# Attention scores from 32-row tiles instead of 64-row tiles with zero queries

## The chip, the cores and the metric

The kernel runs on one core of one Trainium2 chip. The metric is the device time of one execution in microseconds (us). Before the change it is 827.35 us, the median of three runs (826.49 to 828.32). A profile is one such execution, recorded instruction by instruction.

The engines are named as the profile names them: PE is TensorE (matmuls; PEld its weight loads), DVE is VectorE, ACT is ScalarE, POOL is GpSimd, SP is SyncE, which issues most DMAs. PE multiplies a stationary operand (the weights, here up to 128 rows by 128 columns) with a moving operand of up to 512 columns, and writes into PSUM. The array can be split: a matmul with a tile position uses only some rows (a row tile) or only some columns (a column tile), and matmuls on different rows or columns can run at the same time.

## The reference

The input x has 2048 rows of 512 numbers, in bf16. The result is a mix, row by row, of an attention block and a feed-forward block:

```python
def _A_ref(x, wqkv, wo):                       # H = 32 heads, Dh = 16
    qkv = (x @ wqkv).reshape(B, S, 3, H, Dh).transpose(2, 0, 3, 1, 4)
    q, k, v = qkv[0], qkv[1], qkv[2]
    scores = jnp.einsum("bhqd,bhkd->bhqk", q, k) * (Dh ** -0.5)
    p = softmax(scores, axis=-1)
    o = jnp.einsum("bhqk,bhkd->bhqd", p, v)
    return o.transpose(0, 2, 1, 3).reshape(B, S, D) @ wo

def _B_ref(x, w_gate, w_up, w_down):           # 1792 hidden columns
    return (silu(x @ w_gate) * (x @ w_up)) @ w_down

g = sigmoid((x * gate_w).sum(-1, keepdims=True))
return g * a + (1 - g) * b
```

32 heads of 2048 x 2048 scores make 134 million exponentials; that is most of the work outside of PE.

## The kernel before

**Units and tiles.** A unit is four heads (a group g of 8) times one block of 512 queries (qb of 4): 32 units, in the order of the list UNIT. Keys come in 16 tiles of 128 (KT). For one unit and one tile of keys there are four score products, one for each head: 128 keys by 512 queries, a full PSUM bank each. A score tile has keys on the partitions, so that the exponentials can go straight into the product with the values.

**The operands of a score product.** The tile kaug holds the keys of a group, four heads in four strips of 32 partitions: head j in rows 32j to 32j+31. In a strip, row 0 is set to ones, 16 rows hold the head's keys, and the rest is filler that meets zeros. The queries have the same strips; row 0 carries a bound for each query, by which the scores are lowered so that the exponential can't overflow. The queries are stored twice, as variants v = 0 and v = 1 (the second index of q): variant v has the strips of the heads with j % 2 = v, and zeros in the strips of the others. This holds for the tiles q0, q0a, q1 and qx. They are filled in that way by q_pieces, bound_pieces (lines 522 to 611) and variants (575 to 588), none of which the change touches.

**Which products there are.** score (line 719) emits one of them. emit_pair (732) emits two, into the two banks of a tile s_t: heads 0 and 2, or heads 1 and 3 (HEADS at line 717 is 0, 2, 1, 3). ACT then takes the exponential of the whole tile, 128 x 1024, into e_t. There are two s_t tiles in turn. emit_d (765) emits a single one into a tile d_t, in one of three PSUM banks that the rest of the work shares; DVE takes its exponential with a chain of bitwise and arithmetic instructions into y_t, four heads in the order 0, 2, 1, 3. ACT has 841 pairs, DVE 366 single products (91 tiles of keys with all four heads, and two heads of one more).

**The other matmuls.** All the large ones between the scores are split into four column tiles of 128 rows by 32 columns, which run together: the products with the values (pv, line 891, into o_ps), the projections, the feed-forward block (gu, dps, ops). I call four of these one column product. Only two output tiles at the end (two_banks, line 391, tiles a_l_a and a_l_b) use row tiles of 64 rows.

**The order.** Every engine executes in the order in which the program emits (ordered, line 146). That order is laid out while the program is built, by a plan with fixed costs: spend (302) adds 0.216 us to the planned PE time for each pair, single score product or column product, and 0.1 us when the shape changes between rows ("R") and columns ("C"); ACT_US (755) is the planned time of an exponential. In the loop from line 1455 on, the program emits the next pair as soon as its s_t is planned to be free, and fills the time until then with column products and d_t products. Units and their side work have due times (Pacer, 48).

In the profile, every matmul has line 158 (the helper mm), every DVE instruction of the loop line 170, every ACT instruction line 161, so groups are told apart by their tiles: s_t, d_t, e_t, y_t, o_ps and so on.

Of the kernel before, what the change touches and what calls it, by code (L numbers as in the profile page):

```python
# [79 lines left out]
def kernel(  # L80
# [76 lines left out]
    def mm(*args, **kw):  # L157
        return ordered(nc.tensor.matmul(*args, **kw))  # L158
# [360 lines left out]
    def get_q(qb, g):  # L519
        return q1 if g == 1 else qx[(qb * (NB - 1) + g // 2 - 1) % 2][:, :, g % 2, :]  # L520
# [198 lines left out]
    def score(ps, b):  # L719
        n, j = b // 4, HEADS[b % 4]  # L720
        (qb, g), kt = UNIT[n // KT], n % KT
        r = slice(64 * (j // 2), 64 * (j // 2) + 64)
        q = (q0a if n < KT // 2 else q0[qb])[r, j % 2, :] if g == 0 else get_q(qb, g)[r, j % 2, :]
        mm(ps, lhsT=kaug[r, g, kt * P:(kt + 1) * P], rhs=q, start=True, stop=True,
           tile_position=(64 * (j // 2), 0))

    s_end = [0.0, 0.0]
    e_end = {}
# [3 lines left out]
    def emit_pair(bs):  # L732
        i = pairs[0] % 2
        s_t = ps_s.tile([P, 2 * QBW], F32, tag="s", name="s_t")
        e_t = etp.tile([P, 2 * QBW], BF16, tag="e", name="e_t")
        for k, b in enumerate(bs):
            score(s_t[:, k * QBW:(k + 1) * QBW], b)
            e_of[b] = e_t[:, k * QBW:(k + 1) * QBW]
        spend("R", 1, s_end[i])
        flush_act()  # L740
        ready = plan.pe + 0.27

        def exp():
            act(out=e_t[:], in_=s_t[:], func=ACT.Exp, scale=inv_sqrt_dh)
            plan.act = max(plan.act, ready) + ACT_US
            s_end[i] = plan.act + 0.2
            for b in bs:
                e_end[b] = plan.act + 0.27
        exps.append((ready, exp))
        for b in bs:  # L750
            e_left[b] = pairs[0]
        pairs[0] += 1
# [12 lines left out]
    def emit_d():  # L765
# [5 lines left out]
        vcur["i"] += 1  # L771
        d_t = m_tile("d_t")
        score(d_t[:, :], 4 * n + i)
        spend("R", 1)
        e_of[4 * n + i] = y[:, i * QBW:(i + 1) * QBW].bitcast(BF16)
# [819 lines left out]
```

## Time and profile before

| | before |
|---|---|
| median of the runs | 827.35 us (826.49 to 828.32) |
| span of the profiled execution, first to last instruction | 827.2 us |
| ACT busy | 808.9 us (98%) |
| DVE busy | 796.7 us (96%) |
| PE busy | 786.0 us (95%), 8124 matmuls |
| exponentials on ACT (e_t) | 841, mean length 1102 ns |
| score matmuls | 2048, of which 1682 into s_t and 366 into d_t |
| mean granted PE clock | 0.996 |

How to read it: busy time is the time in which at least one instruction of the engine is recorded as running. Neighbouring instructions of an engine overlap in the record, so the busy time of a group is less than its count times its mean length, and the distance from start to start tells what one more of them costs. The length of a matmul has its way through the array in it. The granted clock is the share of PE's full clock that the chip lets through; it is listed with its times. In the list of groups, the number behind the second bar is the idle time of the engine in front of the group's instructions, and behind the arrow stands what ended it. An s_t matmul that waits for ACT e_t waits for its PSUM tile to be read; an e_t that waits for PE s_t waits for its scores.

### The profile page before, as it was taken

Reading aid. Unit: us, or ns where it says so; the run is one execution under the profiler, and the core shown is the slowest. Engines: PE = TensorE matmul, PEld = TensorE weight load, DVE = VectorE, ACT = ScalarE, POOL = GpSimd, SP = SyncE. Lnnn points to the kernel's source line nnn. Section 1 sums busy time; section 2 is a strip of 40 time slices with the busy share of each in tenths; the row PEclk is TensorE's granted clock in tenths of the full one; section 3 lists DMA queues with packets and bytes.
Section 4 is the critical chain, followed back from the end, with each engine's and each line's share of the span. In section 5 each row is a group of like instructions: output and inputs, shape, how many; then the busy total and the mean of one; then the engine's idle time right before and its main releaser. Section 6 shows DMA issues by size and latency. Waiting matters only on the chain. (4 is left out here: it accounts for less than half of the span.)

```text
span 827.2 us, 20410 instructions
## 1 busy us (share of the span) xinstructions
PE 786.0 (95%) x8124; PEld 231.5 (28%) x8125; DVE 796.7 (96%) x1180; ACT 808.9 (98%) x910; POOL 105.5 (13%) x124
## 2 busy tenths in 40 slices
PE   8999999999999999899999999899999999899997
PEld 3322332222222222222222222222222222222222
DVE  6899999999999999999999999999999999999996
ACT  6999999999999999999999999999999999999996
POOL 5010111010111110110111111001011011111110
PEclk9999999999999999999999999999999999999999
DMA  8034346575543445464434555544344545534341
GB/s 178 14 75 90 60 84 125 120 154 104 106 97 64 84 99 126 94 125 94 84 75 90 109 126 110 116 77 95 79 93 88 116 104 115 111 62 83 81 101 48
DMA packets 101095, 79.75 MB, mean 96 GB/s; under 512 B 75744, under 2 KB 89032, under 8 KB 101000
## 3 DMA queue, kind: packets, MB, share of 16 engines
q0 software_dynamic: 12960, 47.19, 30.9%
q1 hardware_dynamic: 86312, 30.93, 15.8%
q8 instruction: 63, 1.03, 0.5%
q10 hardware_dynamic: 1728, 0.33, 0.2%
q14 instruction: 32, 0.26, 0.1%
HBM read 21.55 MB, written 2.35 MB: 29 GB/s over the span
## 5 line engine op out<-in xcount | busy, mean ns | idle before, releaser
L161 ACT ACTIVATE e_t<-s_t 128x1024 bf16<-128x1024 f32 x841 | 784.5, 1102 | 4.1 <-PE s_t L158 3.4
L158 PE MATMUL s_t<-qx,kaug 64*128 64x512 bf16 x1334 | 275.6, 384 | 23.9 <-ACT e_t L161 20.2
L170 DVE TENSOR_SCALAR y_t<-d_t 128x512 uint16<-128x512 f32 x366 | 238.7, 682 | 3.1 <-PE d_t L158 2.4
L158 PEld LDWEIGHTS <-kaug 64*128 64x128 bf16 x2048 | 110.2, 93 | 336.2 <-issue 326.0
L158 PE MATMUL o_ps<-e_t,vaug 128*32 128x512 bf16 x1682 | 168.7, 391 | 0.6 <-DVE osb L170 0.4
L158 PE MATMUL d_t<-qx,kaug 64*128 64x512 bf16 x298 | 101.9, 380 | 2.4 <-DVE y_t L170 0.9
L816 POOL DMA_DIRECT2D y_t<-u_t x45 | 46.8, 1039 | 351.8 <-PE s_t L158 231.7
L158 PEld LDWEIGHTS <-vaug 128*32 128x32 bf16 x2048 | 50.3, 93 | 124.1 <-issue 123.1
L816 POOL DMA_DIRECT2D y_t<-kaug x39 | 41.5, 1063 | 282.5 <-PE s_t L158 145.7
L158 PE MATMUL gu<-xT,wg 128*32 128x512 bf16 x896 | 76.2, 383 | 1.2 <-DMA wg<-in_B_w_gate_dram 0.6
L158 PE MATMUL gu<-xT,wu 128*32 128x512 bf16 x896 | 73.8, 382 | 0.0
L170 DVE TENSOR_SCALAR y_t<-y_t 128x2048 uint16<-128x2048 uint16 x92 | 62.7, 682 | 2.8 <-DMA y_t<-wd_t 1.1
L170 DVE TENSOR_SCALAR z_t<-y_t 128x2048 uint16<-128x2048 uint16 x92 | 63.0, 685 | 1.1
L158 PE MATMUL ops<-wd_t,mt 128*32 128x512 bf16 x672 | 56.7, 383 | 0.0
L170 DVE TENSOR_TENSOR u_t<-u_t 128x2048 f16<-128x2048 f16 (+1 forms) x46 | 55.5, 1207 | 0.9
L170 DVE TENSOR_TENSOR u_t<-u_t,z_t 128x2048 f16<-128x2048 f16 (+1 forms) x46 | 55.4, 1204 | 0.2
L170 DVE TENSOR_TENSOR kaug<-kaug 128x2048 f16<-128x2048 f16 x40 | 48.9, 1221 | 0.9
L170 DVE TENSOR_TENSOR kaug<-kaug,z_t 128x2048 f16<-128x2048 f16 x40 | 48.6, 1216 | 0.1
L158 PE MATMUL s_t<-q,kaug 64*128 64x512 bf16 x208 | 42.3, 383 | 2.7 <-ACT e_t L161 2.4
L170 DVE SCALAR_TENSOR_TENSOR mt<-gs,gu 128x512 bf16<-128x512 bf16 x56 | 38.2, 682 | 2.5 <-PE gu L158 0.2
L170 DVE SCALAR_TENSOR_TENSOR gs<-th,gu 128x512 bf16<-128x512 bf16 x56 | 38.1, 680 | 0.3
L161 ACT ACTIVATE th<-gu 128x512 bf16<-128x512 f32 x56 | 37.4, 668 | 0.0
(148 smaller groups left out, 570.8 us busy)
## 6 DMA issues: line engine op xcount, KB each, us to landing
y_t<-u_t POOLq DMA_DIRECT2D x45, 512.0 KB, 5.0
y_t<-kaug POOLq DMA_DIRECT2D x39, 512.0 KB, 5.0
wg<-in_B_w_gate_dram SPq DMA_DIRECT2D x56, 128.0 KB
wu<-in_B_w_up_dram SPq DMA_DIRECT2D x56, 128.0 KB
y_t<-wd_t POOLq DMA_DIRECT2D x6, 512.0 KB, 5.0
on<-osb SPq DMA_DIRECT2D x120, 16.0 KB
rb<-rr SPq DMA_DIRECT2D x15, 128.0 KB
wd_t<-in_B_w_down_dram SPq DMA_DIRECT2D x7, 256.0 KB
```

The lines of the kernel that those rows point to most:

```text
L158: return ordered(nc.tensor.matmul(*args, **kw))
L161: ordered(nc.scalar.activation(*args, **kw))
L170: return lambda *a, **kw: ordered(f(*a, **kw))
L816: nc.gpsimd.dma_start(out=ya, in_=ua, accum_op=ALU.add)
```

## The change

Each score product takes only the 32 rows of its own head, of the keys and of the queries, and is placed on the row tile of 32 rows at these rows. Before, it took the 64 rows of two heads (heads 0 and 1, or 2 and 3), with zeros in the other head's strip of the queries. The result is the same sum without the zero terms. The queries' variants, their zeros and the DMAs that fill them stay as they are: head j still reads variant j % 2. The pairs, the order and the costs of the plan stay too.

```diff
     def score(ps, b):
         n, j = b // 4, HEADS[b % 4]
         (qb, g), kt = UNIT[n // KT], n % KT
-        r = slice(64 * (j // 2), 64 * (j // 2) + 64)
+        r = slice(32 * j, 32 * j + 32)
         q = (q0a if n < KT // 2 else q0[qb])[r, j % 2, :] if g == 0 else get_q(qb, g)[r, j % 2, :]
         mm(ps, lhsT=kaug[r, g, kt * P:(kt + 1) * P], rhs=q, start=True, stop=True,
-           tile_position=(64 * (j // 2), 0))
+           tile_position=(32 * j, 0))
```

So the two products of a pair lie on rows 0 to 31 and 64 to 95, or on 32 to 63 and 96 to 127, where they took the two halves of the array before.

## The prediction

> **What bounds the kernel now.** I read the busy shares first, then the costliest groups, then who waits for whom, then the matmuls in order of time, and last the granted clock over short stretches. The first two are on the page:
>
> ```profile
> PE 786.0 (95%) x8124; PEld 231.5 (28%) x8125; DVE 796.7 (96%) x1180; ACT 808.9 (98%) x910; POOL 105.5 (13%) x124
> ...
> PEclk9999999999999999999999999999999999999999
> ...
> L161 ACT ACTIVATE e_t<-s_t 128x1024 bf16<-128x1024 f32 x841 | 784.5, 1102 | 4.1 <-PE s_t L158 3.4
> L158 PE MATMUL s_t<-qx,kaug 64*128 64x512 bf16 x1334 | 275.6, 384 | 23.9 <-ACT e_t L161 20.2
> ...
> L158 PE MATMUL d_t<-qx,kaug 64*128 64x512 bf16 x298 | 101.9, 380 | 2.4 <-DVE y_t L170 0.9
> ```
>
> Three engines are full. ScalarE's exponentials set the pace: 841 of them in 784.5 us, 0.93 us each, with 4.1 us of idle time in front of all of them together. So almost nothing can be won in front of ScalarE, but whatever makes the score tiles late is paid there. TensorE is idle for 827.2 - 786.0 = 41 us, much of it by waiting for ScalarE; its order is fixed when the program is built, and the change touches none of the costs from which it is built, so I take the order of instructions as the same.
>
> Next, what a turn of score products costs on TensorE. In the timeline of the matmuls (start, length, operation, count):
>
> ```profile
> 303.13 0.40 PE L158 MATMUL o_ps<-e_t,vaug 128*32 128x512 bf16 x4
> 303.36 0.39 PE L158 MATMUL gu<-xT,wg 128*32 128x512 bf16 x4
> 303.68 0.39 PE L158 MATMUL s_t<-q,kaug 64*128 64x512 bf16 x2
> 304.00 0.40 PE L158 MATMUL gu<-xT,wg 128*32 128x512 bf16 x4
> 304.22 0.60 PE L158 MATMUL gu<-xT,wu 128*32 128x512 bf16 x8
> ```
>
> Read starts, not lengths. Two column products (four tiles of 128 rows by 32 columns) follow each other after 0.22 to 0.23 us. A pair of scores between column products takes 0.32 us on either side: 0.22 of streaming and 0.10 for each change of shape. The pair's two matmuls start together, because they hold different halves of the rows.
>
> Last, the clock. It is full from 5.6 us to the tail except for one stretch. These are three neighbouring stretches of 3.41 us, the length of that gap in the clock (busy us of PE, PEld, DVE, ACT, POOL, then the granted clock), and the matmuls of the first one:
>
> ```profile
> 142.16:145.58 3.42, 2.18 (x16) 0.77 (x15) 3.32 (x7) 3.09 (x4) 0.00 (x0) 1.00 0.07 19
> 145.58:148.99 3.41, 3.41 (x27) 1.04 (x26) 3.34 (x6) 2.46 (x3) 0.99 (x1) 0.50 0.08 20
> 148.99:152.40 3.41, 3.41 (x41) 0.91 (x39) 2.71 (x4) 3.10 (x4) 0.00 (x0) 1.00 0.99 155
> ```
> ```profile
> 142.04 0.39 PE L158 MATMUL s_t<-qx,kaug 64*128 64x512 bf16 x2 [0.25 <-ACT e_t L161]
> 142.37 0.40 PE L158 MATMUL o_ps<-e_t,vaug 128*32 128x512 bf16 x4
> 142.99 0.37 PE L158 MATMUL d_t<-qx,kaug 64*128 64x512 bf16 x1 [0.23 <-DVE gs L170]
> 143.00 0.58 PE L158 MATMUL s_t<-qx,kaug 64*128 64x512 bf16 x2
> 143.79 0.40 PE L158 MATMUL gu<-xT,wg 128*32 128x512 bf16 x4 [0.20 <-DVE mt L170]
> 144.39 0.37 PE L158 MATMUL d_t<-qx,kaug 64*128 64x512 bf16 x1 [0.20 <-DVE y_t L170]
> 144.40 0.58 PE L158 MATMUL s_t<-qx,kaug 64*128 64x512 bf16 x2
> ```
>
> The stretch in which TensorE worked least is followed by one at clock 0.50. The price is in ACT's column: 3.41 - 2.46 = 0.95 us lost in the slow stretch and 3.41 - 3.10 = 0.31 in the next, 1.26 us that a full ScalarE never makes up.
>
> **The change, part by part.** It adds and removes no instruction, DMA or wait. Each of the 2048 score matmuls (1682 into s_t, 366 into d_t) keeps its 512 columns and 128 outputs and goes from 64 rows to 32.
>
> *The duration of one.* No 32-row matmul is in the trace. By rows of other heights: 384 ns (64 rows) and 391 ns (128 rows, o_ps); weight loads 93 ns (64 rows by 128 columns) and 97 ns (128 by 128). Twice the rows cost 7 and 4 ns, so half of them saves 0 to 7 ns; I take 0. A pair still starts together: its heads (0, 2) or (1, 3) lie on different strips.
>
> *Turns within a visit to the score shape.* A d_t product holds half of the rows and must take turns with one of a neighbouring pair: 143.00 shows it, 0.58 us for the pair instead of 0.39. With strips of 32 rows it collides only with its own head. The timeline has 789 visits, of which 282 hold more than one pair or a d_t beside a pair. With the heads as the code deals them out (d_t in the order 0, 2, 1, 3), and no waits, these visits need 1149 turns now and 979 then: 170 x 0.22 = 37 us of TensorE. In the trace, only 99 products start some 0.22 us behind a product of the same half but another strip: 22 us is the value I take, 0 and 37 the ends. The gain falls to an engine that then waits for ScalarE, as s_t already does for 23.7 us in the list of waits. On the end of the kernel it is worth at most what ScalarE loses to s_t, 3.4 us in 7 waits. Of these, 1.6 us (3 waits) lie between 136 and 150 us, around the slow stretch, and I leave them; 1.8 us is the gain, 0 to 3.4 the ends. d_t also comes sooner to VectorE, which waits 2.4 us for it and is 96% busy, beside ScalarE and not behind it: 0.
>
> [...]
>
> [...]
>
> *The filled share of the array, and the clock.* This decides. I laid the 3.41 us grid over the whole trace (the start of the slow stretch and the fall of the clock in the tail, 824.8 us, both lie on it) and summed for each stretch the streaming time, 0.213 us a product, in two ways: as time with any product in the array, and weighted with rows x columns of 128 x 128. A column product and a pair count 1 either way; a lone d_t counts 1 as time and a half as filling. The stretch at 142.16 has 0.41 as time and 0.34 as filling. The lowest stretches after which the clock stayed full have 0.46 as time (346.9 us) and 0.41 as filling (814.5 us). So the clock falls below a limit between 0.41 and 0.46 if time counts, between 0.34 and 0.41 if filling counts; the trace fits both. They part with the change: a pair fills a half instead of all, a d_t a quarter. The mean filling of the 239 stretches goes from 0.66 to 0.52, and 10 stretches come under 0.34, 15 under 0.374 (the middle), 23 under 0.41. One of them is the slow stretch of now, so 9, 14 or 22 are new.
>
> [...]
>
> Between the two ways no row decides. I take filling, because the clock is granted to the array and half of it will carry nothing; that is a judgement, at a little over even. Price of a new slow stretch: 1.26 us measured; the ends are 0.95 (that stretch alone) and 1.71 (half of 3.41, nothing hidden). Sum: 14 x 1.26 = 17.6 us; ends 9 x 0.95 = 8.6 and 22 x 1.71 = 38. What the turns save doesn't help there, since the work that fills the array is the same whoever takes turns; their 1.8 us and the seams' 0.3 I set off within the rounding.
>
> The sum is made against the profiled span, 827.2 us, which is within 0.2 of the median of the runs (827.35, from 826.49 to 828.32), so I add nothing for what lies around it: 827.2 + 17.6 = 845 us, with ends 836 and 865.
>
> **Rivals.** *Time counts, and the strips pay off (faster).* The clock stays, 22 us of turns go, and ScalarE's 1.8 us with them: 827.2 - 1.8 + 0.3 = 825.7, at best 827.2 - 3.4 = 823.8. For it: the 0.20 us turn at 143.00 can be seen, and the waits are there. Against it: ScalarE is full, and shorter turns also shorten the busy time of a stretch. It decides if no stretch falls under 0.41 to 0.46 of time.
>
> *Time counts, and nothing comes of it (same).* The seven waits of ScalarE have other causes, or one or two of the stretches now near 0.50 of time lose a turn (0.22 of 3.41 us is 0.06) and fall under the limit: 827.2 - 1.8 + 1.26 = 826.7; with four of them, 830.4, already slower.
>
> *The 32-row shape costs more for each visit (slower for another reason).* For instance a longer change of shape, or weights that load later. TensorE has 41 us of idle time in 789 visits, so up to 52 ns a visit are covered, and beyond it each visit's excess is paid in full: at 0.10 us, another change of shape, 79 - 41 = 38 us, 865 us. For it: no row shows the shape. Against it: heights of 64 and 128 rows differ by 4 and 7 ns.
>
> **How the numbers follow.** Filling decides, 845 us: 0.52. Another cost of the shape: 0.10. Time counts and faster: 0.18; same: 0.15; slower through new slow stretches: 0.05. Against the bound of 0.2% (1.7 us, about what a measurement of this kernel can tell from no change) that is faster 0.18, same 0.15, slower 0.67. The range goes from 825, which takes in nearly all of the two cases near 827, to 866, the upper ends of both slower cases; what lies outside is the better half of the faster case and a price above these ends.
>
> **What would show it.** Right: the clock at 0.50 in some 10 to 25 stretches of 3.41 us, each behind one with a low filling, and ScalarE's idle time in front of e_t up by about 1 us for each. The turns: pairs beside a d_t of another strip with 0.39 us instead of 0.58, and more time of s_t waiting for ScalarE. Wrong: a full clock behind stretches filled to 0.23 or 0.3, which would make time the measure; or visits of a pair that take more than 0.32 us on either side at full clock, which would be the third rival.

## The result, and the profile after

The changed kernel takes 854.17 us, the median of four runs (850.77 to 859.44), against 827.77 us beside it (826.49 to 828.32): a ratio of 1.033, with a 95% interval from 1.029 to 1.038. The profiled execution took 850.96 us, of which 848.9 are its span, 21.7 us more than the span before. In the ratios here and in the table below, executions that took over 1.5% longer than the fastest of their kernel are left out (one of all32, one of thirdstrip, two of onlypairs32); the medians and ranges have all of them.

From the page of the changed kernel, the lines that answer to those of before (busy us of each engine, its share of the span and its instructions; the granted clock in tenths, in 40 equal slices, where 9 is 0.9 or more; then groups with their count, busy us, mean ns of one, and idle time in front of them):

```profile
PE 799.8 (94%) x8124; PEld 232.2 (27%) x8125; DVE 798.8 (94%) x1180; ACT 813.0 (96%) x910; POOL 103.7 (12%) x124
...
PEclk9999968799989999799999999999999999699999
...
L161 ACT ACTIVATE e_t<-s_t 128x1024 bf16<-128x1024 f32 x841 | 789.1, 1110 | 22.3 <-PE s_t L158 19.4
L158 PE MATMUL s_t<-qx,kaug 32*128 32x512 bf16 x1334 | 272.5, 391 | 30.5 <-ACT e_t L161 28.1
...
L158 PE MATMUL d_t<-qx,kaug 32*128 32x512 bf16 x298 | 101.5, 386 | 3.6 <-DVE y_t L170 0.9
```

The work is the same, instruction for instruction, and none of the groups of 100 and more matmuls grew by more than 34 ns on the mean: s_t from 384 to 391 ns, with the slow stretches in it. But the clock has holes, and ScalarE's idle time in front of e_t has gone from 4.1 to 22.3 us, nearly all of it in wait for s_t. At the same time s_t waits longer for ScalarE than before (28.1 against 20.2 us in this row). TensorE is faster than needed most of the time, and too slow in the holes.

Here is one hole: five neighbouring stretches of the changed kernel (busy us of PE, PEld, DVE, ACT, POOL, then the granted clock; the last two numbers, of the DMA, play no part), and the matmuls of the first of them.

```profile
339.02:342.43 3.41, 2.80 (x26) 0.98 (x26) 3.34 (x6) 3.41 (x5) 0.99 (x1) 1.00 0.66 130
342.43:345.84 3.41, 3.22 (x28) 0.74 (x21) 3.41 (x6) 2.91 (x4) 0.86 (x1) 0.50 0.34 70
345.84:349.26 3.42, 3.42 (x27) 0.62 (x29) 2.75 (x5) 2.93 (x5) 0.00 (x0) 0.50 0.95 163
349.26:352.67 3.41, 3.41 (x34) 0.78 (x28) 1.82 (x2) 1.77 (x2) 0.00 (x0) 0.50 0.39 89
352.67:356.08 3.41, 2.69 (x38) 0.92 (x41) 2.41 (x4) 2.98 (x4) 0.00 (x0) 1.00 0.46 105
```
```profile
339.17 0.39 PE L158 MATMUL s_t<-qx,kaug 32*128 32x512 bf16 x2
340.08 0.39 PE L158 MATMUL s_t<-qx,kaug 32*128 32x512 bf16 x2 [0.53 <-ACT e_t L161]
340.40 0.40 PE L158 MATMUL o_ps<-e_t,vaug 128*32 128x512 bf16 x4
340.74 0.39 PE L158 MATMUL d_t<-qx,kaug 32*128 32x512 bf16 x1
341.00 0.39 PE L158 MATMUL s_t<-qx,kaug 32*128 32x512 bf16 x2
341.32 0.40 PE L158 MATMUL gu<-xT,wg 128*32 128x512 bf16 x4
341.65 0.38 PE L158 MATMUL d_t<-qx,kaug 32*128 32x512 bf16 x1
341.92 0.39 PE L158 MATMUL s_t<-qx,kaug 32*128 32x512 bf16 x2
```

The page calls PE busy for 2.80 of 3.41 us in the first stretch, because its bars overlap (a bar is 0.39 us long where the next product can start after 0.22). By streaming time (0.213 us a product: half of the 0.427 us that lies between the starts of full-size products from 1.7 to 4.2 us of both profiles, where they follow each other at half the later rate) it is 0.56 of the stretch, by filling 0.34, since the four pairs count a half each and the two single products a quarter. The clock falls to 0.50 behind it, and stays there for three stretches. ACT loses 0.50, 0.49, 1.64 and, at full clock again, 0.43 us. The whole execution has 20 slow stretches in front of the tail, in seven holes of 1, 1, 3, 3, 3, 4 and 5. The profiled execution of before had one; of the 25 other executions of it whose mean clock is on record, 24 have 0.999 or 1.000, so most have none.

### The profile page after: what moved, and what is told of

It reads as the page before. It is cut to its first block, busy times and chain, and to the rows that moved or that the text cites. A ratio compares the mean times of both kernels' runs of the same rounds, so it can differ in the third digit from the quotient of the medians.

```text
span 848.9 us, 20407 instructions
## 1 busy us (share of the span) xinstructions
PE 799.8 (94%) x8124; PEld 232.2 (27%) x8125; DVE 798.8 (94%) x1180; ACT 813.0 (96%) x910; POOL 103.7 (12%) x124
## 4 chain that ended last, share of the span: by engine, by line
PE 38%; ACT 29%; DVE 23%; issue 7%; DMA 2%; SPq 0%; DVEq 0%; ACTq 0%
ACT e_t L161 27%; PE s_t L158 13%; DVE y_t L170 9%; PE o_ps L158 7%; PE gu L158 6%; DVE u_t L170 4%; DVE kaug L170 4%; PE d_t L158 4%; PE kp L158 2%; DVE z_t L170 2%; PE ops L158 2%; ACT th L161 2%; DVE mt L170 1%; PE qp L158 1%; DVE gs L170 1%
## 5 line engine op out<-in xcount | busy, mean ns | idle before, releaser
L161 ACT ACTIVATE e_t<-s_t 128x1024 bf16<-128x1024 f32 x841 | 789.1, 1110 | 22.3 <-PE s_t L158 19.4
L158 PE MATMUL s_t<-qx,kaug 32*128 32x512 bf16 x1334 | 272.5, 391 | 30.5 <-ACT e_t L161 28.1
L158 PEld LDWEIGHTS <-kaug 32*128 32x128 bf16 x2048 | 110.4, 91 | 360.0 <-issue 353.1
L158 PE MATMUL o_ps<-e_t,vaug 128*32 128x512 bf16 x1682 | 173.7, 403 | 0.3 <-ACT e_t L161 0.2
L158 PE MATMUL d_t<-qx,kaug 32*128 32x512 bf16 x298 | 101.5, 386 | 3.6 <-DVE y_t L170 0.9
L158 PE MATMUL gu<-xT,wg 128*32 128x512 bf16 x896 | 80.4, 402 | 0.4 <-DMA wg<-in_B_w_gate_dram 0.4
L158 PE MATMUL gu<-xT,wu 128*32 128x512 bf16 x896 | 78.8, 406 | 0.0
L158 PE MATMUL s_t<-q,kaug 32*128 32x512 bf16 x208 | 44.0, 407 | 3.3 <-ACT e_t L161 3.2
```

Source lines behind the costliest of these rows:

```text
L161: ordered(nc.scalar.activation(*args, **kw))
```

## The experiments

Two kinds were run: matmuls by themselves, and the block with parts of the change. The times of the second kind are in the table behind them.

### Matmuls by themselves

**fill**: stages of products with different parts of the array in use.

```diff
+    full(60, "w_a")                       # 128 rows x 128 columns
+    rows(80, 64, (0, 1), "r64x2")         # two row tiles of 64
+    rows(80, 32, (0, 2), "r32x2")         # row tiles of 32: two, then one, three, four
+    cols(80, 32, (0,), "c32x1")           # column tiles of 32: one, then two, four
```

> Not the block: only bf16 products of 512 moving columns, in stages of 80 turns with all 128 rows x 128 columns (filling 1.0) in between; the output is no result of the block. TensorE streams without a pause in every stage, so busy time is 1.0 throughout. Stages and their filling: two row tiles of 64 (1.0), two of 32 (0.5), one of 64 (0.5), one of 32 (0.25), three of 32 (0.75), four of 32 (1.0), one column tile of 128 x 32 (0.25), two (0.5), four (1.0). Theory filling: the clock falls to 0.50 in exactly two stages, one tile of 32 rows and one column tile of 32 columns (0.25 is under the 0.34 to 0.41 of the trace before), and stays full in the others; the turns of a stage go from 0.22 to 0.43 us where it falls. Rival time: the clock stays full throughout, since no stage has an idle TensorE. Rival rows (only the number of active rows counts): it falls with one tile of 32 rows and not with one column tile.

Measured: neither. Each product got a new PSUM tile and so waited for the one before it; one product took 0.64 us from start to start in all stages, and the span was 773.4 us. The page gives a granted clock of 1.00, and that is a trap. The profile before lists 1.00 for its first 5 us too, where products of this size start 0.427 us apart and take up to 634 ns; its first clock entry is at 5.6 us, and behind it, from 7.7 to 9.9 us, they start 0.215 us apart and take 376 to 379. So 1.00 can also mean that no change of the clock is on record, and here none is. The row of the full-size products tells the speed: 583 ns, against 377 to 391 ns in the block, so by their length the clock was at a half from beginning to end (in fill2 below, where its changes are recorded, products of 512 columns follow each other after 0.43 us at half clock and 0.22 at full). A full product every 0.64 us streams 0.213 us at full speed, a third of the time, and the clock did not come up.

```profile
L26 PE MATMUL w_a<-mov 128*128 128x512 bf16 x60 | 35.0, 583 | 6.2 <-DMA mov<-in_A_x_dram 2.8
```

**duty**: k pairs of row tiles, then a wait for ScalarE.

```diff
+    for i in range(k):
+        for j, s in enumerate(strips):
+            mm(ps[j][:, :], lhsT=mov[r, 0:P], rhs=mov[r, :], tile_position=(h * s, 0), ...)
+    nc.scalar.activation(out=junk[:], in_=ps[-1][:, :], func=ACT.Copy)
```

> Not the block either: turns of k pairs of row tiles, then a wait for ScalarE to read the last bank (about 1 us, by the 0.6 to 0.7 us of a 512-column instruction and the ways between the engines), over and over; the output is no result of the block. k pairs stream 0.216 k us. k = 4, 5 and 7 are run with 64 rows and with 32: the same busy time, about 0.46, 0.52 and 0.60 of a turn, at half the filling. Theory filling: with 64 rows the clock holds at k = 4, 5 and 7 (0.46 and more) and falls or wavers at k = 3 (0.39); with 32 rows it falls at k = 4, 5 and 7 (0.23, 0.26, 0.30), still at 10 (0.34), and holds at 20 (0.41), with 14 (0.38) on the edge. Rival time: 32 and 64 rows hold or fall at the same k.

It had the same waits between its products (0.64 us from pair to pair, span 1568.8 us, no change of the clock), so it says nothing on the question. Both were repeated with one PSUM tile for each stage.

**fill2**

> Not the block: the stages of the run fill again, with one PSUM tile for each stage, so that the products stream without waits; the output is no result of the block. TensorE is busy throughout. Filling of the stages: two row tiles of 64 (1.0), two of 32 (0.5), one of 64 (0.5), one of 32 (0.25), three of 32 (0.75), four of 32 (1.0), one column tile of 128 x 32 (0.25), two (0.5), four (1.0), each of 80 turns, with full products in between. Theory filling: the clock falls to 0.50 in exactly two stages, one tile of 32 rows and one column tile (0.25 is under the limit near 0.36), and stays full in the others. Rival time: full throughout, since no stage has an idle TensorE. Rival rows (only the number of active rows counts): it falls with one tile of 32 rows and not with one column tile.

Measured, in the order 32 rows x2, 64 x1, 32 x1, 32 x3, 32 x4, one column tile, two column tiles (busy us of PE, PEld, ACT, POOL, then the clock):

```profile
46.00:61.00 15.00, 15.00 (x143) 7.81 (x139) 0.00 (x0) 0.00 (x0) 1.00 0.01 1
72.00:87.00 15.00, 15.00 (x71) 6.57 (x70) 0.00 (x0) 0.00 (x0) 1.00 0.01 1
102.00:128.00 26.00, 26.00 (x62) 8.97 (x61) 0.00 (x0) 0.00 (x0) 0.50 0.00 0
146.00:161.00 15.00, 15.00 (x213) 8.08 (x210) 0.00 (x0) 0.00 (x0) 1.00 0.00 1
172.00:187.00 15.00, 15.00 (x287) 8.26 (x280) 0.00 (x0) 0.00 (x0) 1.00 0.01 2
199.00:214.00 15.00, 15.00 (x71) 6.78 (x70) 0.00 (x0) 0.00 (x0) 1.00 0.00 0
229.00:244.00 15.00, 15.00 (x142) 7.87 (x140) 0.00 (x0) 0.00 (x0) 1.00 0.00 1
```

TensorE is busy without a pause in every line, and the clock falls in one: single products of 32 rows (third line, 0.50). A single column tile of 128 rows by 32 columns (sixth line, 1.00) has the same area and keeps the clock. So time is refuted, and so is the area that I had written down as filling: in these stages **rows count, columns don't**. In the block the two are the same number, since its column tiles run four at a time; the rival that I had named last is the right form of the theory.

**duty2**

> Not the block: k pairs of row tiles, then a wait for ScalarE to read the last bank, over and over, again with one PSUM tile for each stage; the output is no result of the block. k pairs stream 0.216 k us, the wait adds about 0.95. With 64 rows k is 3, 4, 5, 7 (busy share 0.41, 0.48, 0.53, 0.61, filling the same); with 32 rows 4, 5, 7, 10, 14, 20 (busy 0.48, 0.53, 0.61, 0.69, 0.76, 0.82, filling half of that). Theory filling: with 64 rows the clock holds at all k; with 32 rows it falls at 4, 5 and 7 (0.24, 0.27, 0.31), is on the edge at 10 (0.35) and holds at 14 and 20 (0.38, 0.41). Rival time: both heights hold or fall at the same k.

Measured for k = 7, 64 rows first, then 32:

```profile
185.00:240.00 55.00, 38.20 (x319) 17.36 (x319) 13.71 (x23) 0.00 (x0) 1.00 0.00 1
422.00:502.00 80.00, 65.20 (x290) 23.63 (x291) 12.08 (x21) 0.00 (x0) 0.50 0.00 1
```

The same products for each wait keep the clock with 64 rows and lose it with 32. With 64 rows it held at all four k, down to a share of 0.42 on the average (k = 3: 3 x 0.216 of 1.55 us a turn) and 0.375 in its thinnest stretches of 3.41 us. With 32 rows it fell at all six. That it fell at 14 and 20 too was not expected: on the average they have 0.39 and 0.41, but the falls came behind single thin stretches. One that holds a whole wait of 0.90 us has (3.41 - 0.90) / 3.41 x 0.5 = 0.37 at most; the stretch in front of the fall had 0.364 in both, and with k = 20 it took 17 us until one came. And once down it did not come back: it is 0.50 over the 55 to 112 us that were read of each of the six. Pairs of 32 rows at half clock offer at most a quarter (half of the rows at half the speed, an estimate).

### The block with parts of the change

The kernels of this group share one edit ahead of the loop: the transposed x is made by products with the identity instead of by transposing DMAs. base64 is the kernel before with this edit, all32 the changed kernel with it.

> The kernel before with one difference ahead of the loop, which the three runs beside it share: the transposed x comes from TensorE products with the identity instead of from transposing DMAs. The loop is the same, so this is the base for those three. All theories: 0 to 15 us more than the kernel before, all of it in the first 30 us; the clock full behind that, but for 0 to 3 stretches.

> The whole change on that base. All theories: the difference of the change itself, 22 to 32 us above base64, with 15 to 30 slow stretches of 3.41 us.

| run | median us (range) | ratio to the kernel before [95%] | slow stretches in the loop, profiled execution |
|---|---|---|---|
| base64 | 840.56 (840.19 to 841.44) | 1.016 [1.015, 1.018] | 1 |
| all32 | 864.71 (860.00 to 881.54) | 1.044 [1.040, 1.047] | 16 |
| onlypairs32 | 888.17 (875.58 to 899.91) | 1.066 [1.057, 1.074] | 25 |
| onlysingle32 | 857.39 (856.15 to 858.94) | 1.036 [1.034, 1.038] | 2 |
| warm32 | 851.32 (848.81 to 855.19) | 1.028 [1.026, 1.031] | 10 |
| thirdstrip | 845.00 (843.56 to 856.29) | 1.021 [1.020, 1.022] | 5 |
| thirdstrip64 | 855.74 (851.89 to 861.30) | 1.035 [1.032, 1.038] | 19 |

thirdstrip and thirdstrip64 ran together on another chip than the other five; the kernel before took 827.82 us beside them, against 826.80 beside base64 and all32.

The base costs 13.8 us more than the kernel before (840.56 against 826.80 beside it), and the change on it 24.2 us, close to the 26.4 us of the change itself. So the base is good for comparisons.

**onlypairs32**

```diff
-    def score(ps, b):
+    def score(ps, b, h=32):
-        r = slice(32 * j, 32 * j + 32)
+        r = slice(h * (32 * j // h), h * (32 * j // h) + h)
...
-           tile_position=(32 * j, 0))
+           tile_position=(r.start, 0))
...
-        score(d_t[:, :], 4 * n + i)
+        score(d_t[:, :], 4 * n + i, 64)
```

> On that base, the pairs into s_t with 32 rows, the single products into d_t with 64. Theory filling: by the 3.41 us grid on the trace of before, with pairs counted at a half, 8 stretches come under 0.36 to 0.374 (15 with the whole change, of which 20 slow ones came), so some 8 to 12 slow stretches at 1.1 us: 9 to 15 us above base64, half of the whole change. Visits that hold both heights change shape inside, 282 of them at 0.10 us or more, mostly into TensorE's idle time; that may add a few us. Rival cost of the 32-row shape: nearly all of the whole change, 20 us and more, at a full clock. Rival shortened turns (the clock follows time, and the turns that vanish make the stretches too short): a 64-row product still collides with one of the pair, so no slow stretches and no change, 0 to 3 us.

**onlysingle32**

```diff
-            score(s_t[:, k * QBW:(k + 1) * QBW], b)
+            score(s_t[:, k * QBW:(k + 1) * QBW], b, 64)
```

> On that base, the single products into d_t with 32 rows, the pairs with 64. Theory filling: the grid has 1 to 3 stretches under the limit, where before has 1: 0 to 3 us above base64, plus what the changes of height inside 282 visits cost (0.10 us each, if they drain as rows to columns do: 28 us of TensorE time, most of it into 41 us of idle time, 0 to 8 us at the end). Rival cost of the 32-row shape: a share of the whole change by count, 366 of 2048 products, 5 us, at a full clock. Rival shortened turns: none, as no turn vanishes.

Both missed, and on the same term. The single products alone cost two thirds of the whole change, and pairs alone are slower than all of it (their fastest execution takes 875.6 us, three of the four of all32 at most 865.2). What I had put into TensorE's idle time is on the path: the change of height within a visit (a seam). In the timeline of onlysingle32, two visits (one pair and one single product each) and what follows:

```profile
300.38 0.39 PE L158 MATMUL d_t<-q,kaug 32*128 32x512 bf16 x1
300.70 0.39 PE L158 MATMUL s_t<-qx,kaug 64*128 64x512 bf16 x2
301.02 0.62 PE L158 MATMUL dps<-wd_t,mt 128*32 128x512 bf16 x8
301.57 0.39 PE L158 MATMUL s_t<-qx,kaug 64*128 64x512 bf16 x2
301.89 0.38 PE L158 MATMUL d_t<-q,kaug 32*128 32x512 bf16 x1
302.20 0.40 PE L158 MATMUL o_ps<-e_t,vaug 128*32 128x512 bf16 x4
```

From a product of 32 rows to one of 64 it takes 0.32 us, as from rows to columns: 0.10 more than the 0.22 between two column products. What TensorE does in the 0.10 us, no run shows. A visit with one pair and one single product takes 0.64 us until the next column product, against 0.53 in base64 and, in all32, 0.32 or 0.53 by the strip. By the medians of the visits' kinds that is 164 x 0.10 + 50 x 0.22 = 27 us of TensorE time. onlysingle32 takes 16.8 us more than base64, with one slow stretch more in the loop and one more in the first 25 us. That leaves most of the 16.8 us for the seams, though no run has the seams alone. In onlypairs32 the same 27 us meet the clock. My reading, which no run shows by itself, is that what delays TensorE thins out the rows per stretch, and that at half clock the loop with its seams rarely gets enough together to be let up: its longest hole is 58 us, 17 stretches. The order of the two theories can't be read from this pair, since the seams are in both; the next three runs were made for that.

**warm32**: all32 with more of the dummy products that the program has for idle TensorE time.

```diff
-        work_at.append((plan.pe, mms))
+        work_at.append((plan.pe, mms * fill))     # 0.5 for a pair, 0.25 for a single product
...
-                    w for t, w in work_at[-24:] if t > plan.pe - 3.0) < 6.5:
+                    w for t, w in work_at[-24:] if t > plan.pe - 3.0) < 8.0:
...
-                    mm(o_of[closed][32 * j:32 * j + 16, :], lhsT=vaug[:, 0, G * 4 * VC:], ...
+                    mm(o_of[closed][32 * j:32 * j + 32, :], lhsT=zcol[:, :], ...
```

> all32 with the dummy product of line 1486 let loose: its rule counts pairs at 0.5 and single products at 0.25, acts under 8.0 instead of 6.5, and the product fills 128 columns (zero weights, added into o_ps, so the result is the same). The plan then puts in 69 of them, 0.22 us of TensorE each and 0.10 us for each change of shape that it brings, where it expects TensorE to idle. Theory filling: they lift the emptiest stretches by 0.06 each, so fewer slow stretches than in all32, half or less, and 8 to 20 us less time. Rival cost of the 32-row shape: more work on TensorE, the same time or 5 to 15 us more than all32. Rival time: each lifts the busy time as well, but by the same 0.06; it differs from filling only through fill2 and duty2.

13.4 us less than all32 with 69 dummies more: within the expected range. The number of slow stretches went from 16 to 10, where half was expected. It speaks for the clock, but not for rows against time, since a dummy adds to both.

**thirdstrip**: a third product beside the pair, on rows that are idle anyway.

```diff
+        i = j ^ 1                                  # the strip beside the pair's first head
+        r = slice(32 * i, 32 * i + 32)
...
+        mm(o_of[closed][:, :], lhsT=kaug[r, g, kt * P:(kt + 1) * P], rhs=q[r, ...],   # zero queries
+           start=False, stop=False, tile_position=(32 * i, 0), skip_group_check=True)
```

> all32 with work added: beside 667 of the 841 pairs runs a third product of 32 rows on one of the two empty strips, 512 columns long, with keys from that strip and queries that are zero there; it adds zeros into o_ps, so the result is the same. It starts with the pair and so takes no turn of its own; it costs a weight load of 128 columns and a no-operation that waits for the third product before it. The 32-row shape, the pairs and the turns are those of all32. Theory filling (share of active rows): these pairs fill 0.75 instead of 0.5, the mean share goes from 0.52 to 0.57, by the grid 3 to 5 stretches come under 0.36 to 0.374 instead of 12 to 15; so 3 to 8 slow stretches and 845 to 856 us, 9 to 20 us less than all32 (864.7) in spite of the added work. Rivals cost of the shape and time: nothing won, and more by the price of 667 more products and waits, 865 to 890 us.

**thirdstrip64**: its control.

```diff
-        mm(o_of[closed][:, :], ..., rhs=q, ...)
+        mm(o_of[closed][:, 0:64], ..., rhs=q[:, 0:64], ...)
```

> The control to thirdstrip: the same instructions, but the third product is only 64 columns long, so it adds an eighth of the filling (0.03 instead of 0.25 to such a pair). Theory filling: as many slow stretches as all32 or a few more (16 to 25), 862 to 885 us, and clearly slower than thirdstrip although it does less work. Rivals: as fast as thirdstrip or faster.

This decides. thirdstrip does more work than all32, in the same shapes and turns, and is faster: 845.0 against 864.7 us, in the range that filling gave and 20 us from that of the rivals. The third product takes no turn of its own; it starts with the pair, and the next column product still comes 0.32 us behind the pair:

```profile
300.11 0.39 PE L158 MATMUL s_t<-qx,kaug 32*128 32x512 bf16 x2
300.12 0.38 PE L158 MATMUL o_ps<-qx,kaug 32*128 32x512 bf16 x1
300.43 0.61 PE L158 MATMUL dps<-wd_t,mt 128*32 128x512 bf16 x8
```

With the third product cut to an eighth of its length it is 855.7 us, 10.7 us slower while it does less. Five of the six executions of thirdstrip take 843.6 to 845.3 us at mean clocks of 0.982 to 0.987, the sixth 856.3 at 0.966; the six of the control take 851.9 to 861.3 at 0.956 to 0.973. The clock on the pages and the exponentials, all32 first, then thirdstrip and thirdstrip64:

```profile
PEclk8999995889999999999999999999999997999999
...
L161 ACT ACTIVATE e_t<-s_t 128x1024 bf16<-128x1024 f32 x841 | 789.7, 1122 | 21.1 <-PE s_t L158 16.0
```
```profile
PEclk8999999799999999999999999999999999999999
...
L161 ACT ACTIVATE e_t<-s_t 128x1024 bf16<-128x1024 f32 x841 | 786.6, 1115 | 8.1 <-PE o_ps L158 4.6
```
```profile
PEclk8999995999989999999999999989999979888999
...
L161 ACT ACTIVATE e_t<-s_t 128x1024 bf16<-128x1024 f32 x841 | 789.6, 1124 | 20.5 <-PE s_t L158 17.3
```

Two things stay open. The control came out below its range (862 to 885) and below all32 in the median, though its profiled execution has the same span (858.1 us) and 19 slow stretches against 16; the slow stretches of a kernel differ from run to run, and I can't tell their spread from a gain of the added 64 columns. And thirdstrip stays 4.4 us above base64: five slow stretches instead of one, at the 1.0 us that one costs in the changed kernel (below), are about worth that, but its added waits were not measured apart.

### One limit for all of them

I laid the grid of 3.41 us stretches (in the profiles before and after, all changes of the clock in the loop lie on such a grid: the slow pieces last 3.41, 10.24, 13.65 or 17.07 us) over eleven profiled executions (both kernels, the block's seven variants, fill2 and duty2; without the first 20 and the last 14 us) and gave each stretch its share of active rows: the streaming time of a product at full speed x its rows / 128, column tiles that run together counted once. Of 2487 stretches, 263 were followed by a slow one. The limit that tells best which is 0.365, and it is wrong for 18; the best limit on the time in which anything streams is 0.50 and is wrong for 97. Most of the 263 were slow themselves. Of the stretches at full clock, some 2200, 39 were followed by a slow one: there the limit of 0.365 rows is wrong for 7, and the best limit on time for 36, hardly better than to say that the clock never falls. In the changed kernel alone, the seven stretches at full clock behind which it fell had 0.27 to 0.38, and the lowest behind which it stayed had 0.384 (shares to some 0.02, by how the products at the edges of a stretch are counted, so the two touch); by time they are mixed, 0.46 to 0.57 against 0.52 and more. In a slow stretch the same limit tells best whether the next is full again, if work counts as it would at full speed: by my estimate from it, that is nearly three quarters of a slow stretch with all rows streaming (0.365 / 0.5). In the changed kernel this is not sharp: it stayed slow with shares up to about 0.37 and came back with shares from about 0.35 on.

## Why the prediction was right, and where it was off

**What bounds the kernel**: right. ScalarE was the engine that paid, with 17.6 of the 21.7 us as idle time.

**The duration of one product, 0**: right. From the last column product to the pair and from the pair to the next one it takes 0.31 and 0.32 us at full clock in both traces.

**Turns, 22 us of TensorE and 1.8 us on the end**: right in kind. Products that start some 0.2 us behind one of the same half fell from 205 to 107, those of another strip among them from 99 to 18. (The 1149 and 979 turns of the prediction are those of all 789 visits, not of the 282; their difference of 170 stands.) In the changed kernel a pair and two single products can start at once:

```profile
442.65 0.39 PE L158 MATMUL s_t<-qx,kaug 32*128 32x512 bf16 x2
442.65 0.39 PE L158 MATMUL d_t<-qx,kaug 32*128 32x512 bf16 x2
443.35 0.39 PE L158 MATMUL s_t<-qx,kaug 32*128 32x512 bf16 x2 [0.30 <-ACT e_t L161]
```

And the third line shows where it goes: into a wait for ScalarE. Outside of the slow stretches, the first 20 and the last 15 us, ScalarE's idle time fell from 2.1 to 1.1 us, so the gain is 1.0 us.

**Seams at the tail, 0.3 us**: no run shows this term of the sums by itself. What the trace after shows in its place: a_l_a at 831.29 us and the pair behind it at 831.61 are 0.32 us apart, where it was 0.23 before. ScalarE's idle time in the last 15 us rose by 0.15 us.

**Filling and the clock, 14 new slow stretches at 1.26 us**: right in taking filling and not time, though as rows, not as rows x columns. The prediction had chosen it by judgement, at 0.52, with no row to decide; now it is shown. The sizes were off in both directions. There were 19 new stretches in the profiled execution, but only six new holes: I had counted 14 falls of one stretch each, and five of the seven holes last three stretches or more; my reading is that the same limit has to be met at half the speed. So 14 came near 19 by luck, from too many falls that were each taken as too short. ScalarE's idle time in the slow stretches and the microsecond behind each hole rose from 1.3 to 20.3 us, so a new one costs 1.0 us. What the sum left out is 4.1 us of ScalarE's busy time: an exponential that follows other work without a pause adds 0.92 us to it, one behind a pause its whole 1.02, and 47 had a pause in front of them instead of 13, which makes some 3.5 of the 4.1. Together: 19.0 in the slow stretches, -1.0 outside, -0.4 in start and tail, and 4.1 make the 21.7 us of the span.

The predicted 845 us stands against 851 of the profiled execution and a median of 854. Of the 6 us to the profiled execution, 4.1 are in the span (21.7 instead of 17.6) and 2.0 are a slip of the sum: in every run whose span is on record the time is 1.8 to 2.1 us longer than the span, and I had added nothing, because the span of 827.2 happened to lie at the median of the runs. It was the span of an execution with a slow stretch, which most executions of that kernel don't have. The 3 us from there to the median are the clock again: the four executions have mean clocks of 0.959, 0.956, 0.947 and 0.943, which is some 20 to 28 slow stretches, and go from 850.8 to 859.4 us, about 1.1 us for each.

**The rivals.** Both cases in which time counts are refuted by fill2 and duty2, and in the block by thirdstrip and its control. The cost of the 32-row shape is refuted by the visits' 0.32 us at full clock. But that rival's price stood on a cover that onlysingle32 shows to be too large: 27 us of added TensorE time, 35 ns a visit, came with 17 us more, most of them not from the clock, where I had 52 ns a visit as free. The idle time of TensorE, which waits and is waited for, was not a reserve that could be spent anywhere.

## What to carry to other kernels

Before you give matmuls fewer rows, sum the active rows per 3.41 us stretch, not the busy time, in the places where TensorE already waits: in these runs the clock went to 0.50 behind stretches with rows x streaming time under some 0.37 (0.365 tells it best, wrong for 18 of 2487), and what paid was the engine that waits for TensorE (ScalarE, with 17.6 of the 21.7 us). Zeros that fill idle rows can be the cheaper choice (827.77 against 854.17 us), and idle rows can also be filled by a product beside the real one (thirdstrip, 845.0 us, against 864.7 of all32). And keep one height of row tile within a run of products: each change cost what a change from rows to columns does, 0.10 us here.

## What was not expected of the hardware

- In fill2 the clock goes with the rows and not with the columns: single products of 32 rows x 128 columns run at 0.50, single ones of 128 rows x 32 columns at 1.00, both without a pause.
- As far as these runs tell, the limit is the same on the way up, counted in work at full speed (0.365 over the eleven executions; not sharp in the changed kernel, 0.35 to 0.37). None of the six loops of 32-row pairs in duty2 came back from 0.50.
- fill ran at half clock from beginning to end, by the length of its products (583 ns for 512 columns, against 377 to 391 in the block), and its profile shows a granted clock of 1.00.
- From 32-row to 64-row tiles and back TensorE takes 0.32 us from start to start in onlysingle32, 0.10 more than the 0.22 of two column products, as from row to column tiles.
